# One output copy of each group moves from ScalarE to VectorE, and one low part of the last batch moves two slots earlier

## The chip, the core and the metric

The kernel runs on one core of a Trainium2 chip. Its time is the device time of one execution in microseconds (us). Engines go by the names of the profile: PE is TensorE (PEld its weight loads), ACT is ScalarE, DVE is VectorE, POOL is GpSimd, and SP is SyncE, which issues the DMAs here.

## What is computed

An attention with 32 inducing points over four batches of 12544 tokens of 128 channels, and a maxout layer on its result. Cut to what matters:

```python
def mab(q, kv):
    s = scale * (q @ kv.transpose(0, 2, 1))
    s = s - s.max(-1, keepdims=True)
    a = np.exp(s)
    a /= a.sum(-1, keepdims=True) + 1e-09
    return a @ kv
h = mab(I, x)            # 32 rows a batch
y = mab(x, h)            # as many rows as tokens
# then, with w1, w2, w3 of 128 x 768 and w_out of 768 x 128
h = np.maximum(np.maximum(y @ w1, y @ w2), y @ w3)
return h @ w_out
```

## The kernel before

A batch has 98 tiles of 128 tokens. They are taken in seven groups: one short group of two tiles and six full groups of 16. A full group is worked as four chunks `q` of 512 columns (a short one as one chunk of 256), so that a batch has 25 chunks and the program 100, numbered `c.n`. Each chunk has six slots `j`, one for each 128 of the 768 hidden channels: 600 slots in all, 24 for a full group. In this text a slot of a full group is numbered from 0 to 23 within it, and a stretch runs from the start of the first matmul of a group's slot 0 to that of the next group. There are 24 such stretches, six a batch.

The largest of three products is made with w2's product taken off: with weights `w1 - w2` PE makes a matmul into `pu` (L790), with `w3 - w2` one into `pv` (L800), ACT makes `ru`, the relu of `pu` (L809), DVE makes `h`, the larger of `pv` and `ru` (L830). What was taken off comes back through `w2 @ w_out`, once a chunk (L861). The second product, `h` by `w_out`, is made in two parts for accuracy: ACT rounds `h` to `hi` (L819), and `lows` is the rest, `h - hi`, made by POOL (L827) or, for a few slots, by DVE (L833). Six slots later PE adds `hi` by both parts of `w_out` and `lows` by the high part into `acc` (L862 to L864, in `stage2`). When a chunk's six slots are in, `finish` copies `acc` to `o` (L875) and SP sends it out (L876).

The order of the instructions is written out by hand. `main` goes through the slots: in each it calls `advance`, then a pending `finish`, then what a plan holds for this slot (steps of the two softmaxes, loads, sums), then `stage2`. `advance` issues for slot s: `pu` of slot s+1, `pv` of s, `ru` of s+1, `hi` of s-1, then on DVE `h` of s and behind it a low part that was put off from the call before, so that the low part of slot k stands behind `h` of slot k+2. A chunk's `finish` comes six slots after its last one; that of the first chunk (`q` = 0) of a full group stands at slot 12 of the group. At slot 2 of each stretch PE makes a burst: scores for the next group (L696), in the last batch for every other group; in batches 1 to 3 also scores and sums of the next batch (L366, L502). The other steps of the softmax stand between slots 3 and 15: DVE L709, L712, L714, L719, L726, L727, the transpose L739 and `pl` L745, ACT L716, L724 and `ph` L742.

`pu`, `pv` and `acc` have two PSUM banks each, `h` has five buffers, `o` three. `LOWVEC` and `LOWLAST` (L120, L121) hold the slots of a group whose low part DVE makes, `LOWLAST` for the last batch. Output copies are ACT's, save those of chunks 0 to 2 and half of the last chunk.

Of the kernel before, what the change touches and what calls it, by code (L numbers as in the profile page):

```python
# [25 lines left out]
def kernel(ctx, tc, x, xt, ind_t, w1, w2, w3, w_out, out):  # L26
    nc = tc.nc
# [90 lines left out]
        (16, 10, "t", 3, 6),  # L118
    )
    LOWVEC = (23, 0, 15, 18)  # L120
    LOWLAST = (23, 0, 9, 15, 18)  # L121
    UW = 2 * DF + C
    UQ = UW // NQ

# [556 lines left out]
    def sorted_(ap):  # L681

        return ap.rearrange("p (b a) -> p a b", a=2)

    def halves(ap):

        return ap.rearrange("p (a b) -> p a b", a=2)
# [147 lines left out]
    class Chunk:  # L835
# [7 lines left out]
        def low(self, k):  # L843
# [3 lines left out]
            if self.b == 0 and self.gi == 1:  # L847
                return NJ * self.q + k in LOWVEC[:1]
            return NJ * self.q + k in (LOWVEC if self.b + 1 < B else LOWLAST)

# [14 lines left out]

    def finish(c):
        at = groups[c.gi]["at"] + (c.q or 0) * c.w
        turns = [(nc.vector.tensor_copy if c.n < 3 else nc.scalar.copy, nc.sync)]
        if len(c.acc) > 1:

            turns = [(nc.vector.tensor_copy, nc.sync), (nc.scalar.copy, nc.scalar)]
        for (acc, cs), (copy, queue) in zip(c.acc, turns):
            o = op.tile([P, 512], F32, name="o", tag="o", bufs=3)
            w = cs.stop - cs.start
            copy(out=halves(o[:, :w]), in_=sorted_(acc[:, :w]))  # L875
            queue.dma_start(out=out[c.b, :, at + cs.start : at + cs.stop], in_=o[:, :w])  # L876
# [120 lines left out]
    def main():  # L997
        over = None
        for s in range(len(slots) + LAG + 1):

            if s >= LAG:
                spare[0] = bank_o[((s - LAG) // NJ + 1) % 2]
            if pipe["next"] <= s:
                advance()
            k = s // NJ + AHEAD
            if s % NJ == 4 and k < len(chunks):
                chunks[k].pT = probs(chunks[k])
            if over:
                finish(over)
                over = None  # L1010
            if s == len(slots) + LAG:
                break
            for f, args in plan[s]:
                f(*[state[a[1]] if isinstance(a, tuple) and a[0] == "state" else a for a in args])
            if s >= LAG:
                c, j = slots[s - LAG]
                stage2(c, j)
                if j == NJ - 1:
                    over = c
# [132 lines left out]
```

## Time and profile before

| | |
|---|---|
| median of 3 runs | 789.68 us (789.67 to 790.14) |
| the profiled execution | 790.35 us, of which the span of its instructions is 788.5 us |
| granted TensorE clock, mean | 0.999 of full speed |
| PE busy | 774.7 us, 98% of the span |
| PE weight loads busy | 626.4 us, 79% |
| ACT busy | 727.1 us, 92% |
| DVE busy | 639.4 us, 81% |
| POOL busy | 639.6 us, 81% |

Busy time is the union of the instructions' times, and an instruction's time includes what it takes to pass through its engine; the next one may start before it ends. A matmul of 512 columns is shown as 0.38 us long, and the next starts some 0.215 us after it. For such engines the distance from one start to the next tells more than the duration. "Idle before" is the time in which an engine had nothing running, with what released it.

### The profile page before, as it was taken

How to read it: one execution, taken by the hardware profiler on the slowest of the kernel's cores; microseconds unless marked ns; L12 is line 12 of the kernel's file. 1: busy time of each engine (PE TensorE's matmuls, PEld its weight loads, DVE VectorE, ACT ScalarE, POOL GpSimd, SP SyncE). 2: the span in 40 equal slices, each digit the busy share in tenths (PEclk: the TensorE clock that was granted, in tenths of full speed). 3: DMA queues.
4: the chain of work that ended last, by engine and by line, in shares of the span. 5: the costliest groups of instructions: out<-in, count | busy, mean ns of one | idle time of the engine just before them, and what ended most of it. 6: DMA issues, size and time to landing. Idle time of an engine off the chain costs nothing.

```text
span 788.5 us, 14348 instructions
## 1 busy us (share of the span) xinstructions
PE 774.7 (98%) x4567; PEld 626.4 (79%) x4567; DVE 639.4 (81%) x1071; ACT 727.1 (92%) x1529; POOL 639.6 (81%) x523
## 2 busy tenths in 40 slices
PE   8999999999999999999999999999999999999998
PEld 6768878878787787787878877878888788787887
DVE  5898978878877787887887878878888788888876
ACT  5789899999998999998998999999999999999996
POOL 1379879878788897887987978879879989888887
PEclk9999999999999999999999999999999999999999
DMA  9744325274542643543644336334223222222221
GB/s 355 293 148 126 100 91 178 62 249 161 189 139 65 200 131 101 188 123 108 217 137 132 114 103 195 120 114 134 71 79 96 74 81 81 68 87 73 69 81 53
DMA packets 52266, 102.24 MB, mean 130 GB/s; under 512 B 18144, under 2 KB 21344, under 8 KB 46944
## 3 DMA queue, kind: packets, MB, share of 16 engines
q1 hardware_dynamic: 52048, 101.21, 40.5%
q8 instruction: 36, 0.59, 0.3%
q14 instruction: 38, 0.31, 0.1%
q10 hardware_dynamic: 144, 0.13, 0.0%
HBM read 48.12 MB, written 25.69 MB: 94 GB/s over the span
## 4 chain that ended last, share of the span: by engine, by line
PE 56%; ACT 33%; POOL 3%; DMA 3%; DVE 2%; issue 1%; SPq 0%; POOLq 0%; ACTq 0%; DVEq 0%
ACT ru L809 14%; ACT hi L819 13%; PE pu L790 10%; PE acc L862 9%; PE pv L800 9%; PE acc L863 9%; PE acc L864 9%; PE aux L696 3%; POOL lows L827 3%; ACT o L875 2%; PE acc L502 2%; DMA raw<-in_w_dram 2%; PE aux L366 2%; PE acc L861 2%; ACT aux L449 1%
## 5 line engine op out<-in xcount | busy, mean ns | idle before, releaser
L827 POOL TENSOR_TENSOR lows<-h,hi 128x512 fp32r<-128x512 f32 (+1 forms) x504 | 624.4, 1275 | 112.4 <-ACT hi L819 109.3
L830 DVE TENSOR_TENSOR h<-pv,ru 128x512 f32<-128x512 f32 (+1 forms) x600 | 400.9, 673 | 123.8 <-PE pv L800 63.0
L809 ACT ACTIVATE ru<-pu 128x512 f32<-128x512 f32 (+1 forms) x600 | 407.0, 679 | 37.8 <-PE pu L790 37.5
L819 ACT CAST hi<-h 128x512 fp32r<-128x512 f32 (+1 forms) x596 | 416.3, 699 | 0.3 <-DVE h L830 0.2
L790 PE MATMUL pu<-pT,us 128*128 128x512 f32 (+1 forms) x600 | 229.2, 382 | 4.5 <-ACT ru L809 3.7
L800 PE MATMUL pv<-pT,us 128*128 128x512 f32 (+1 forms) x600 | 226.6, 378 | 1.6 <-DVE h L830 1.5
L862 PE MATMUL acc<-hi,wo_hi 128*128 128x512 f32 (+1 forms) x594 | 225.5, 380 | 0.0
L863 PE MATMUL acc<-hi,wo_lo 128*128 128x512 f32 (+1 forms) x594 | 222.6, 375 | 0.0
L864 PE MATMUL acc<-lows,wo_hi 128*128 128x512 f32 (+1 forms) x594 | 222.6, 375 | 0.0
L790 PEld LDWEIGHTS pu<-pT,us 128*128 128x128 f32 x600 | 113.2, 189 | 37.8 <-ACT ru L809 18.8
L862 PEld LDWEIGHTS acc<-hi,wo_hi 128*128 128x128 f32 x594 | 112.2, 189 | 21.9 <-issue 7.5
L800 PEld LDWEIGHTS pv<-pT,us 128*128 128x128 f32 x600 | 113.4, 189 | 19.6 <-DVE h L830 6.6
L864 PEld LDWEIGHTS acc<-lows,wo_hi 128*128 128x128 f32 x594 | 112.3, 189 | 15.3
L863 PEld LDWEIGHTS acc<-hi,wo_lo 128*128 128x128 f32 x594 | 112.3, 189 | 14.7
L833 DVE TENSOR_TENSOR lows<-h,hi 128x512 fp32r<-128x512 f32 x96 | 87.7, 913 | 0.8 <-ACT hi L819 0.8
L875 ACT COPY o<-acc 128x512 f32<-128x512 f32 (+1 forms) x96 | 65.3, 680 | 0.0
L861 PE MATMUL acc<-pT,us 128*128 128x512 f32 (+1 forms) x99 | 37.3, 376 | 0.0
L502 PEld LDWEIGHTS acc<-xg,aT 128*32 128x32 f32 x640 | 18.0, 110 | 9.6 <-issue 5.4
L696 PE MATMUL aux<-xT,hT 128*32 128x512 f32 x192 | 25.1, 603 | 0.0
L366 PE MATMUL aux<-xT,iT 128*32 128x512 f32 x184 | 24.1, 596 | 0.2 <-ACT pT L768 0.2
L502 PE MATMUL acc<-xg,aT 128*32 128x128 f32 x640 | 21.4, 273 | 0.1
L861 PEld LDWEIGHTS acc<-pT,us 128*128 128x128 f32 x99 | 18.7, 189 | 2.6 <-DVE hs L540 0.2
(163 smaller groups left out, 445.6 us busy)
## 6 DMA issues: line engine op xcount, KB each, us to landing
out_dram<-o SPq DMA_DIRECT2D x95, 256.0 KB, 2.2
xg<-in_x_dram SPq DMA_DIRECT2D x23, 1024.0 KB, 6.1
xT<-in_xt_dram SPq DMA_DIRECT2D x18, 1024.0 KB, 5.5
pT<-ph SPq DMA_DIRECT2D x190, 64.0 KB, 2.0
pT<-pl SPq DMA_DIRECT2D x190, 64.0 KB, 2.0
raw<-in_w_dram SPq DMA_DIRECT2D x3, 768.0 KB, 8.7
us<-uh SPq DMA_DIRECT2D x24, 52.0 KB, 1.9
us<-ul SPq DMA_DIRECT2D x24, 52.0 KB, 2.5
```

The lines of the kernel that those rows point to most:

```text
L790: nc.tensor.matmul(out=pu[:, :w], lhsT=state[c.b]["us"][:, 2 * j * P : (2 * j + 1) * P], rhs=turned(c.pT[:, :w]), start=True, stop=True,)
L800: nc.tensor.matmul(out=pv[:, : d.w], lhsT=state[d.b]["us"][:, (2 * j + 1) * P : (2 * j + 2) * P], rhs=turned(d.pT[:, : d.w]), start=True, ...
L809: nc.scalar.activation(out=halves(ru[:, :w]), in_=sorted_(pu[:, :w]), func=AF.Relu)
L819: nc.scalar.copy(out=hi[:, : c.w], in_=h[:, : c.w])
L827: nc.gpsimd.tensor_sub(**args)
L830: nc.vector.tensor_max(out=halves(h[:, : d.w]), in0=sorted_(pv[:, : d.w]), in1=halves(relus.pop(s)[:, : d.w]))
L833: nc.vector.tensor_sub(**low)
L861: nc.tensor.matmul(out=to, lhsT=us[:, 2 * DF :], rhs=turned(c.pT[:, cs]), start=True, stop=False)
L862: nc.tensor.matmul(out=to, lhsT=wo_hi[:, row_of(j), :], rhs=turned(c.hh[j][:, cs]), start=False, stop=False)
L863: nc.tensor.matmul(out=to, lhsT=wo_lo[:, row_of(j), :], rhs=turned(c.hh[j][:, cs]), start=False, stop=False)
L864: nc.tensor.matmul(out=to, lhsT=wo_hi[:, row_of(j), :], rhs=turned(c.hl[j][:, cs]), start=False, stop=(j == NJ - 1))
L875: copy(out=halves(o[:, :w]), in_=sorted_(acc[:, :w]))
```

## The change

`finish` lets VectorE copy the output of every chunk with `q` = 0, the first of each full group. In the last batch the slot 9 in the list of low parts on VectorE becomes slot 7: POOL makes that of slot 9, VectorE that of slot 7.

```diff
     LOWVEC = (23, 0, 15, 18)
-    LOWLAST = (23, 0, 9, 15, 18)
+    LOWLAST = (23, 0, 7, 15, 18)
...
     def finish(c):
         at = groups[c.gi]["at"] + (c.q or 0) * c.w
-        turns = [(nc.vector.tensor_copy if c.n < 3 else nc.scalar.copy, nc.sync)]
+        turns = [(nc.vector.tensor_copy if c.n < 3 or c.q == 0 else nc.scalar.copy, nc.sync)]
```

No other engine's order changes than those of ACT and DVE (POOL makes as many subtractions as before). On ACT, a full group in batches 1 to 3, at slot 12 (`pu_81` and `pu_82` are the two banks of `pu`, `acc_86` is one of `acc`):

```order
 L809 ACTIVATE ru<-pu_82 128x512
 L819 CAST hi<-h 128x512
-L875 COPY o<-acc_86 128x512
 L809 ACTIVATE ru<-pu_81 128x512
 L819 CAST hi<-h 128x512
```

The copy is gone from between `hi` and the next `ru`. On DVE, the same place (`aux_79` holds the scores of the next group, `rs` the reciprocal of their sums, `pv_83` and `pv_84` are the banks of `pv`):

```order
 L727 TENSOR_TENSOR aux_79<-aux_79,rs 128x512
 L830 TENSOR_TENSOR h<-pv_83,ru 128x512
+L875 COPY o<-acc_86 128x512
 L830 TENSOR_TENSOR h<-pv_84,ru 128x512
 L739 STREAM_TRANSPOSE aux_79<-aux_79 128x512
```

It stands there behind `h` of slot 12, ahead of `h` of slot 13 and of the transpose of the softmax. On DVE, a group of the last batch, from slot 8 to slot 13:

```order
 L830 TENSOR_TENSOR h<-pv_83,ru 128x512
 L830 TENSOR_TENSOR h<-pv_84,ru 128x512
+L833 TENSOR_TENSOR lows<-h,hi 128x512
 L719 TENSOR_REDUCE rs<-aux_80 128x16
 L830 TENSOR_TENSOR h<-pv_83,ru 128x512
 L830 TENSOR_TENSOR h<-pv_84,ru 128x512
-L833 TENSOR_TENSOR lows<-h,hi 128x512
 L726 RECIPROCAL rs<-rs 128x16
 L727 TENSOR_TENSOR aux_80<-aux_80,rs 128x512
 L830 TENSOR_TENSOR h<-pv_83,ru 128x512
+L875 COPY o<-acc_85 128x512
 L830 TENSOR_TENSOR h<-pv_84,ru 128x512
```

The low part leaves its place behind `h` of slot 11 for one behind `h` of slot 9, and the copy comes in behind `h` of slot 12, as in the other batches.

## Rows read from the trace of the kernel before

**Rows 1.** The page: busy times of PE and its weight loads, and the chain by engine

```profile
PE 774.7 (98%) x4567; PEld 626.4 (79%) x4567; DVE 639.4 (81%) x1071; ACT 727.1 (92%) x1529; POOL 639.6 (81%) x523
...
PE 56%; ACT 33%; POOL 3%; DMA 3%; DVE 2%; issue 1%; SPq 0%; POOLq 0%; ACTq 0%; DVEq 0%
```

**Rows 2.** Who waited for whom: us in total, times, the longest

```profile
PEld pu L790 <- ACT ru L809: 18.8, 49, 0.7
```

**Rows 3.** Two stretches: length, then each engine's busy us (instructions), clock, DMA

```profile
298.41:328.85 30.43, 30.13 (x173) 24.38 (x173) 24.87 (x41) 28.50 (x61) 25.14 (x21) 1.00 0.44 137
...
548.40:577.76 29.36, 29.36 (x169) 24.72 (x169) 24.42 (x42) 28.28 (x59) 25.42 (x21) 1.00 0.24 70
```

**Rows 4.** The chain of waits from 298 to 334: start, us, what

```profile
306.32 0.60 ACT ru L809
...
317.94 0.49 ACT o L875
```

**Rows 5.** Timeline of PE, end of the first stretch: start, us, engine, line, operation

```profile
326.98 0.38 PE L864 MATMUL acc<-lows,wo_hi 128*128 128x512 f32 x1
327.66 0.48 PE L790 MATMUL pu<-pT,us 128*128 128x512 f32 x1 [0.31 <-ACT ru L809]
327.98 0.38 PE L800 MATMUL pv<-pT,us 128*128 128x512 f32 x1
```

**Rows 6.** Groups by form: xcount, busy us, mean ns, idle before

```profile
L875 ACT COPY o<-acc 128x512 f32<-128x512 f32 x93 | 64.1, 689 | 0.0
```

**Rows 7.** Timeline of ACT, the same stretch, at slot 12

```profile
317.75 0.68 ACT L875 COPY o<-acc 128x512 f32<-128x512 f32 x1
318.23 0.70 ACT L809 ACTIVATE ru<-pu 128x512 f32<-128x512 f32 x1
...
320.22 0.70 ACT L742 CAST ph<-aux 128x512 fp32r<-128x512 f32 x1
```

**Rows 8.** Timeline of DVE, the same place

```profile
316.98 0.68 DVE L830 TENSOR_TENSOR h<-pv,ru 128x512 f32<-128x512 f32 x1
317.86 0.69 DVE L830 TENSOR_TENSOR h<-pv,ru 128x512 f32<-128x512 f32 x1 [0.20 <-PE pv L800]
318.47 0.72 DVE L739 STREAM_TRANSPOSE aux<-aux 128x512 f32<-128x512 f32 x1
...
320.02 0.69 DVE L830 TENSOR_TENSOR h<-pv,ru 128x512 f32<-128x512 f32 x1 [0.26 <-POOL lows L827]
```

**Rows 9.** Timeline of DVE, first group: one of its output copies

```profile
64.86 0.68 DVE L875 COPY o<-acc 128x512 f32<-128x512 f32 x1
```

**Rows 10.** Timeline of POOL at that time, merged

```profile
58.82 13.71 POOL L827 TENSOR_TENSOR lows<-h,hi 128x512 fp32r<-128x512 f32 x11
```

**Rows 11.** Timeline of DVE, the last batch, stretch from 640.50

```profile
653.07 0.68 DVE L719 TENSOR_REDUCE rs<-aux 128x16 f32<-128x512 f32 x1
653.67 0.68 DVE L830 TENSOR_TENSOR h<-pv,ru 128x512 f32<-128x512 f32 x1
...
655.23 1.32 DVE L833 TENSOR_TENSOR lows<-h,hi 128x512 fp32r<-128x512 f32 x1
...
657.35 1.28 DVE L830 TENSOR_TENSOR h<-pv,ru 128x512 f32<-128x512 f32 x2
```

**Rows 12.** Timeline of POOL in that stretch, three instructions merged

```profile
652.24 3.76 POOL L827 TENSOR_TENSOR lows<-h,hi 128x512 fp32r<-128x512 f32 x3
```

**Rows 13.** Timeline of PE in that stretch

```profile
655.18 0.38 PE L800 MATMUL pv<-pT,us 128*128 128x512 f32 x1
...
657.34 0.38 PE L790 MATMUL pu<-pT,us 128*128 128x512 f32 x1
658.09 0.48 PE L800 MATMUL pv<-pT,us 128*128 128x512 f32 x1 [0.37 <-DVE h L830]
```

**Rows 14.** Timeline of PE at the program's end

```profile
783.96 0.38 PE L864 MATMUL aux<-lows,wo_hi 128*128 128x256 f32 x1 [0.34 <-POOL lows L827]
```

## The prediction, before the changed kernel was run

> **What bounds the kernel now.** I read the page first, then the waits, the stretches, the chain of one stretch, and the timelines of each engine in it. The page says that PE is busy for 98% of the span [rows 1], which looks like a kernel with nothing left. But a matmul of 512 columns is shown as 0.38 us long while the next starts 0.215 us after it, so that share hides short waits. The other line of the page, the chain that ended last, is one third ACT [rows 1], and PE's weight load for `pu` waits 49 times for ACT's `ru` [rows 2].
>
> Of the 24 stretches of one full group each (24 slots), eight are 30.43 us long; the one from 298.41 to 328.85 stands for them [rows 3]. ACT is busy for 28.50 of its 30.43 us. It idles once, while PE computes scores and sums in a burst, and from 306.32 on the chain runs through ACT, instruction behind instruction, and ACT's output copy at 317.94 lies on it [rows 4]. (The timeline shows the same copy at 317.75; the chain counts it from the end of what precedes it.) The chain leaves ACT where PE must wait: the matmul into `pu` starts 0.68 us after the one ahead of it, where 0.215 us is the pace, and the next needs 0.32 us. PE so loses 0.47 + 0.10 = 0.57 us [rows 5]. `pu` has two banks; PE may not write one until ACT's `ru` has read it. Then PE goes on to the next burst, and the cycle closes. So in these stretches what ACT sheds ahead of that wait shortens the cycle, up to what PE waits.
>
> **The change, part by part.** *The copy leaves ACT.* 23 copies of 128x512 move: one for each of 24 full groups, less that of chunk 1, which VectorE makes already. A copy is shown as 689 ns [rows 6], but the next ACT instruction starts 0.48 us after it (317.75 to 318.23, rows 7), and that is what ACT gains. It is bounded by 0 and 0.48 us a group. For twelve stretches (the eight, the second of batch 1, the fifth of batch 2 and the first of batches 2 and 3) PE's waits exceed 0.48 us, so I take it whole: 12 x 0.48 = 5.76 us. [...]
>
> Of the other stretches of batches 1 to 3, one (548.40) has PE busy without a break [rows 3]; I give it nothing. Four hold fewer of these waits; I take 0.38 us each, the mean of the 49 [rows 2], between 0 and 0.48: 4 x 0.38 = 1.52 us.
>
> *The copy joins VectorE.* It stands behind `h` of slot 12, so it would start at 317.58 where that one starts at 316.98 [rows 8] and the pace of VectorE is 0.60 us. `h` of slot 13 goes from 317.86 to 318.18, the transpose from 318.47 to 318.79. `h` of slot 15 started at 320.02 after an idle time, which takes up what is left: the delay is over. What waits for them? ACT's `ph` would now come at 319.74 rather than 320.22 [rows 7], and the transpose ends at 318.79 + 0.72 = 319.51. So the copy costs nothing here; the margin is 0.23 us, and past it ACT would wait and give the gain back. The copy's input is long done, its output DMA keeps its place on SP, and three `o` buffers cover a shift of tenths.
>
> How long does it last? VectorE made three such copies early on, and the one at 64.86 took 0.68 us [rows 9] while POOL ran eleven subtractions without a gap [rows 10]. That matters because the low part that VectorE computes is slow under POOL: 1.32 us instead of 0.68, ending 0.55 us after POOL's instruction ends at 656.00 [rows 11, 12]. The copy does not wait that way.
>
> *The low part at slot 7 instead of 9, last batch.* In the stretch from 640.50 it stood between `h` of slots 11 and 12, waited for POOL, and with two more instructions behind it `h` of slot 12 came at 657.35. PE's `pv` of slot 14, due 0.215 us after 657.34, started at 658.09: 0.53 us lost, and 0.10 to restart [rows 11, 13]. Now it issues where 653.07 stands, waits for POOL's first instruction of rows 12 (3.76 / 3 = 1.25 us, so to 653.5) and ends near 654.05. `h` of slot 10 goes from 653.67 to 654.6 and ends at 655.3; `pv` of slot 12 was due at 655.18 [rows 13], so PE loses about 0.1 + 0.1 there. Then `h` of slot 12 comes near 656.7, 0.6 us earlier than before; the copy takes that 0.6 us, and `h` of slot 13 is where it was. The old wait of 0.63 is a wait of 0.2. Three of the last six stretches have the old wait; 3 x 0.43 = 1.29 us, between 0 (the wait only moves) and 1.9 us (it goes). Of the others PE has no wait to lose, and 0.48 us of ACT buys nothing there. What is late next in them is PE itself.
>
> *The end.* The last products wait 0.34 us for POOL [rows 14], whose instructions in the last group start after ACT's `hi`; ACT arrives earlier, so I take 0.34 us, between 0 and 0.48.
>
> The sum is 5.76 + 1.52 + 1.29 + 0.34 = 8.91 us. The profiled execution took 790.35 us, 1.85 more than its span; less 8.91 it is 781.44. It lies 0.67 above the median of the three runs, 789.68, so I predict **780.8 us**.
>
> **The rivals.** *Slower: the copy waits for POOL after all.* VectorE's low part is the row for it [rows 11]; against it are the early copies [rows 9, 10]. A wait of half a POOL instruction, 0.64 us, exceeds the margin of 0.23 by 0.41, so a steady stretch gains 0.07 rather than 0.48 us: 0.8 us in all. In eight groups VectorE has no idle time there (two with two softmaxes, six of the last batch), and PE pays the 0.64: 5.1 us. That is 4.3 us slower, 794.0 us. It decides from a copy longer than 0.68 + 0.23 = 0.91 us.
>
> *No change: PE is the bound, as its 98% says.* Its waits would be ones it always has, the time 789.7 us. Against it are the chain through ACT and the lost 0.57 us [rows 4, 5]. [...]
>
> *Half: the next thing in line takes the rest.* If `h` of slot 13 or the transpose runs only some 0.2 us later than I reckon, ACT waits for it in every group. Then 0.24 us a stretch are left, 12 x 0.24 = 2.9 us, and if the last batch's wait only moves and the four others halve (0.8), with the end (0.34) the gain is about 4 us: 785.6 us.
>
> **How the numbers follow.** A measurement of this kernel can tell about 0.2%, 1.6 us, from no change. I give the forecast 0.72, half 0.13, no change 0.06, the slower rival 0.09. Faster by over 0.2% is the first two, 0.85; within it 0.06; slower 0.09. The range begins where the other stretches of batches 1 to 3 also give all 0.48 us, the last batch's waits go, and some of its stretches gain 0.48: 777.5 us. It reaches past the half case, to 786.0, and leaves out no change and slower.
>
> **What would show it.** Steady stretches should be 29.95 us long instead of 30.43, with ACT still the chain and PE's wait before the burst about 0.1 instead of 0.47 us. The VectorE copies should last 0.68 us; a mean over 0.9 means the slower rival. ACT's `ph` should follow its predecessor without idle time. In the last batch the wait of `pv` for `h` should be at slot 12, short, and gone from slot 14. I am wrong if PE's wait vanishes while the stretch keeps its length, or if ACT's idle time during the burst grows by what the copy freed.

## The result, and the profile after

The change made the kernel slower. Its 20 runs have a median of 805.58 us (790.62 to 813.95) beside 790.04 us (789.46 to 790.65) before; the ratio is 1.0079, 95% interval 1.0052 to 1.0106. The ratio is taken over the nine runs nearest the fastest, since a comparison leaves disturbed runs out; here the scatter is the change's own, as the experiments show, so the median of all 20, 2.0% above before, says more. The forecast was 780.8 us.

The profiled execution is the fastest of the 20: 790.62 us, span 788.8 us, beside 790.35 and 788.5 before. So it shows gains and losses that nearly cancel. The page of the changed kernel, the lines that answer to [rows 1]:

```profile
PE 772.5 (98%) x4567; PEld 630.0 (80%) x4567; DVE 662.8 (84%) x1094; ACT 717.5 (91%) x1506; POOL 642.1 (81%) x523
...
PE 86%; ACT 5%; DMA 4%; issue 2%; SPq 1%; DVE 1%; POOL 0%; DVEq 0%; ACTq 0%
```

ACT's third of the chain has gone, as meant. 23 copies left ACT (1529 to 1506 instructions) and joined DVE (1071 to 1094). But DVE's busy time grew by 23.4 us, more than 23 copies at 0.68 us, 15.6. The groups by form show what else grew (xcount, busy us, mean ns, idle before):

```profile
L833 DVE TENSOR_TENSOR lows<-h,hi 128x512 fp32r<-128x512 f32 x96 | 102.7, 1070 | 0.8 <-ACT hi L819 0.8
...
L875 DVE COPY o<-acc 128x512 f32<-128x512 f32 x25 | 17.0, 680 | 0.0
```

Before, VectorE's low parts read so:

```profile
L833 DVE TENSOR_TENSOR lows<-h,hi 128x512 fp32r<-128x512 f32 x96 | 87.7, 913 | 0.8 <-ACT hi L819 0.8
```

There are as many now, but their durations sum to 15.0 us more. (Durations overlap, so this and the copies are more than 23.4.) The waits of the changed kernel (us in total, times, the longest), beside [rows 2]:

```profile
PEld pv L800 <- DVE h L830: 16.3, 28, 2.5
...
ACT hi L819 <- DVE h L830: 7.1, 5, 1.9
...
PEld pu L790 <- ACT ru L809: 5.4, 22, 0.4
PE pv L800 <- DVE mx L434: 4.2, 2, 2.1
```

The wait for ACT's `ru` fell from 18.8 to 5.4 us. In its place PE's weight loads wait 28 times for DVE, for up to 2.5 us (6.6 us in 18 waits before), and ACT five times, for up to 1.9 us. The row that names `mx` (L434) is misleading: that reduction, 0.14 us long, only stands behind the instruction that was late. Three stretches that all took 30.43 us before, and one piece of the last (length, then busy time of PE, PEld, DVE, ACT and POOL, clock, DMA, as in [rows 3]):

```profile
107.19:139.28 32.09, 29.99 (x173) 24.53 (x173) 28.09 (x43) 28.22 (x59) 25.07 (x21) 1.00 0.42 134
139.28:169.18 29.90, 29.90 (x174) 24.59 (x172) 25.64 (x42) 27.87 (x60) 25.30 (x21) 1.00 0.42 137
487.23:521.00 33.77, 31.67 (x173) 25.71 (x173) 28.88 (x43) 29.67 (x62) 26.76 (x22) 0.95 0.41 131
517.36:520.77 3.41, 3.41 (x9) 2.70 (x8) 2.54 (x5) 3.31 (x8) 2.23 (x2) 0.50 0.15 40
```

The second is what was forecast: 29.90 us, PE busy throughout. The first holds one wait of PE of 2.10 us. The third holds the same wait, and 1.2 us after it TensorE's granted clock stood at 0.50 of full speed for 3.41 us. Matmuls followed each other at 0.43 instead of 0.215 us there; 33.77 less 32.09 is what that cost, 1.7 us. Here is what happened in the first stretch, on DVE, POOL, ACT and PE in turn (timeline: start, us, engine, line, operation, and idle time before):

```profile
130.95 0.69 DVE L830 TENSOR_TENSOR h<-pv,ru 128x512 f32<-128x512 f32 x1 [0.27 <-PE pv L800]
131.56 3.94 DVE L833 TENSOR_TENSOR lows<-h,hi 128x512 fp32r<-128x512 f32 x1
135.43 0.68 DVE L830 TENSOR_TENSOR h<-pv,ru 128x512 f32<-128x512 f32 x1
136.03 0.14 DVE L434 TENSOR_REDUCE mx<-mx 128x1 f32<-128x5 f32 x1
...
127.49 7.46 POOL L827 TENSOR_TENSOR lows<-h,hi 128x512 fp32r<-128x512 f32 x6
...
131.48 0.73 ACT L819 CAST hi<-h 128x512 fp32r<-128x512 f32 x1
...
136.14 0.62 ACT L819 CAST hi<-h 128x512 fp32r<-128x512 f32 x1 [1.93 <-DVE h L830]
...
133.68 0.38 PE L790 MATMUL pu<-pT,us 128*128 128x512 f32 x1
136.16 0.48 PE L800 MATMUL pv<-pT,us 128*128 128x512 f32 x1 [2.10 <-DVE mx L434]
```

VectorE's low part of slot 15 takes 3.94 us. POOL meanwhile does those of slots 14, 16 and 17 without a gap (six instructions in 7.46 us, 1.24 us from start to start, the last three from 131.22 to 134.95), and VectorE's ends at 135.50, 0.55 us after POOL's last. This is the delay of 0.55 us that [rows 11] and [rows 12] show, behind three instructions of POOL instead of a part of one. `h` of slot 18 stands behind it on DVE, so ACT's `hi` waits 1.93 us and PE's `pv` loses 2.27 us.

Before, POOL paused at that place. The same stretch of the kernel before, DVE, POOL and ACT:

```profile
132.31 1.17 DVE L833 TENSOR_TENSOR lows<-h,hi 128x512 fp32r<-128x512 f32 x1
...
127.87 5.06 POOL L827 TENSOR_TENSOR lows<-h,hi 128x512 fp32r<-128x512 f32 x4
133.20 2.65 POOL L827 TENSOR_TENSOR lows<-h,hi 128x512 fp32r<-128x512 f32 x2 [0.28 <-ACT hi L819]
...
132.37 0.75 ACT L819 CAST hi<-h 128x512 fp32r<-128x512 f32 x1
```

POOL ended slot 14 at 132.93 and then waited 0.28 us for ACT's `hi` of slot 16. In this pause VectorE's low part got in, and ended at 133.48, again 0.55 us after POOL. Now ACT is some 0.5 us earlier in the stretch: its `hi` of slot 16 ends at 132.21, 25.02 us after the stretch's start (133.12 and 25.53 before). That is 0.28 us before POOL's subtraction of slot 14 ends (132.49), and POOL goes on without a pause.

That alone does not decide it. In the stretch from 139.28 ACT leads as much, and VectorE gets in all the same (DVE, POOL):

```profile
163.62 1.48 DVE L833 TENSOR_TENSOR lows<-h,hi 128x512 fp32r<-128x512 f32 x1
...
160.77 6.71 POOL L827 TENSOR_TENSOR lows<-h,hi 128x512 fp32r<-128x512 f32 x5
```

Let a low part on VectorE that takes 3 us or more, because POOL goes from one subtraction straight to the next, be called a shut-out. The profile of after has four that before does not have (at 131.6, 262.1, 353.1 and 511.6; one more, at 80.7, both have).

### The profile page after: what moved, and what is told of

The parts are those of the page before. It is cut to its first block, busy times and chain, and to the rows that moved or that the text cites. A ratio compares the mean times of both kernels' runs of the same rounds, so it can differ in the third digit from the quotient of the medians.

```text
span 788.8 us, 14395 instructions
## 1 busy us (share of the span) xinstructions
PE 772.5 (98%) x4567; PEld 630.0 (80%) x4567; DVE 662.8 (84%) x1094; ACT 717.5 (91%) x1506; POOL 642.1 (81%) x523
## 4 chain that ended last, share of the span: by engine, by line
PE 86%; ACT 5%; DMA 4%; issue 2%; SPq 1%; DVE 1%; POOL 0%; DVEq 0%; ACTq 0%
PE pv L800 15%; PE acc L862 15%; PE pu L790 15%; PE acc L863 14%; PE acc L864 14%; PE aux L696 3%; PE acc L502 2%; PE aux L366 2%; PE acc L861 2%; ACT ru L809 2%; ACT hi L819 2%; DMA xg<-in_x_dram 1%; DMA pT<-ph 1%; DVE h L830 1%; DMA xT<-in_xt_dram 1%
## 5 line engine op out<-in xcount | busy, mean ns | idle before, releaser
L809 ACT ACTIVATE ru<-pu 128x512 f32<-128x512 f32 (+1 forms) x600 | 391.3, 653 | 40.5 <-PE pu L790 40.2
L819 ACT CAST hi<-h 128x512 fp32r<-128x512 f32 (+1 forms) x596 | 400.8, 673 | 7.6 <-DVE h L830 7.1
L790 PE MATMUL pu<-pT,us 128*128 128x512 f32 (+1 forms) x600 | 226.8, 378 | 0.2
L833 DVE TENSOR_TENSOR lows<-h,hi 128x512 fp32r<-128x512 f32 x96 | 102.7, 1070 | 0.8 <-ACT hi L819 0.8
L875 ACT COPY o<-acc 128x512 f32<-128x512 f32 (+1 forms) x73 | 47.6, 652 | 0.0
```

The costliest lines, as they stand in the source:

```text
L790: nc.tensor.matmul(out=pu[:, :w], lhsT=state[c.b]["us"][:, 2 * j * P : (2 * j + 1) * P], rhs=turned(c.pT[:, :w]), start=True, stop=True,)
L809: nc.scalar.activation(out=halves(ru[:, :w]), in_=sorted_(pu[:, :w]), func=AF.Relu)
L819: nc.scalar.copy(out=hi[:, : c.w], in_=h[:, : c.w])
L833: nc.vector.tensor_sub(**low)
```

## The experiments

The theory: relieving ACT takes away POOL's pause, and VectorE's low part of slot 15 is then shut out in some groups. The rivals: the copy on VectorE delays or disturbs what follows it there; or the low part at slot 7 does. The first four were run on one chip (before: 790.06, 789.71 to 790.74).

**The copy's move alone.** Against the change:

```diff
-    LOWLAST = (23, 0, 7, 15, 18)
+    LOWLAST = (23, 0, 9, 15, 18)
```

> The copy on VectorE, the low part of the last batch back at slot 9. Theory (pause lost): ACT, relieved of the copy, has hi of slot 16 ready before POOL ends slot 14, so POOL goes on without the pause of some 0.3 us in which VectorE's low part of slot 15 used to come in; it is then held off for two or three POOL instructions. Expected: low parts over 2 us in three to six groups of batches 1 to 3, times scattered from about 790 to 815 us as with the change. Rival (the low part at slot 7 does it): no low part over 2 us but the one near 80.6 us that was there before, and about 782 to 784 us.

Measured: 800.23 us (794.32 to 811.63 in four), ratio 1.0103 (1.0064 to 1.0142). The profiled run, the slowest, has eight new shut-outs, more than the three to six expected, and six stretches of 3.41 us at clock 0.50, and its 24 stretches sum to 748.86 us instead of 727.74. The stretch that went well in the profile of after, 163.62, is shut out in this one (DVE, POOL):

```profile
163.91 3.96 DVE L833 TENSOR_TENSOR lows<-h,hi 128x512 fp32r<-128x512 f32 x1
...
161.09 6.23 POOL L827 TENSOR_TENSOR lows<-h,hi 128x512 fp32r<-128x512 f32 x5
```

POOL's five take 6.23 us here and 6.71 there: where VectorE gets in, POOL's next subtraction lasts 1.75 us instead of 1.27.

**The low part alone.** Against the change:

```diff
-        turns = [(nc.vector.tensor_copy if c.n < 3 or c.q == 0 else nc.scalar.copy, nc.sync)]
+        turns = [(nc.vector.tensor_copy if c.n < 3 else nc.scalar.copy, nc.sync)]
```

> The low part of the last batch at slot 7, every output copy where it was before. Theory: batches 1 to 3 as before, no low part over 2 us but the one near 80.6 us, no scatter, and the last batch some 1.3 us shorter: 788 to 789.5 us. Rival (the low part at slot 7 does it): scatter up to 810 us.

Measured: 789.27 us (788.90 to 789.65 in ten), ratio 0.9989 (0.998 to 0.9999). No new shut-out, no scatter: the fault is the copy's half.

**ACT relieved, VectorE not loaded.**

```diff
     def finish(c):
+        if c.q == 0 and c.n >= 3:
+            return
...
-        turns = [(nc.vector.tensor_copy if c.n < 3 or c.q == 0 else nc.scalar.copy, nc.sync)]
+        turns = [(nc.vector.tensor_copy if c.n < 3 else nc.scalar.copy, nc.sync)]
```

> The output of the first chunk of 23 groups is neither copied nor sent, so neither ACT nor VectorE has that work; the low part of the last batch at slot 7. Theory: ACT's relief is what takes POOL's pause, so low parts over 2 us appear in some groups of batches 1 to 3 and the times scatter over more than 5 us, from about 788 up. Rival (VectorE, with one copy more, comes late): no such low part, no scatter, 779 to 782 us.

Measured: 805.78 us (802.0 to 809.77), ratio 1.0199 (1.0161 to 1.0236), with seven new shut-outs and four falls of the clock. On the page:

```profile
L833 DVE TENSOR_TENSOR lows<-h,hi 128x512 fp32r<-128x512 f32 x96 | 107.5, 1120 | 0.8 <-ACT hi L819 0.8
```

23 copies fewer in the kernel (and their output DMAs), and it is 2% slower. No copy stood on VectorE, so the copy there is not the cause; ACT's lead is enough.

**Both engines copy.** VectorE copies as in the change, and ACT copies the same product to a tile that nothing reads:

```diff
             copy(out=halves(o[:, :w]), in_=sorted_(acc[:, :w]))
+            if c.q == 0 and c.n >= 3:
+                o2 = op.tile([P, 512], F32, name="o2", tag="o2", bufs=1)
+                nc.scalar.copy(out=halves(o2), in_=sorted_(acc))
```

> VectorE copies as in the change, and ACT copies the same products too, into a tile that nobody reads; the low part of the last batch at slot 7. Theory: without ACT's relief the pause is there, so no low part over 2 us but the one near 80.6 us, no scatter, 788 to 790.5 us. Rival (VectorE's added copy does it): low parts over 2 us in three to six groups, scatter up to 810 us.

Measured: 800.60 us (800.1 to 801.4), ratio 1.0133 (1.0118 to 1.0149). No new shut-out, no scatter, the clock full throughout: that part held. The time missed, because the edit brought a wait of its own (waits; DVE; ACT):

```profile
ACT o L878 <- DVE o L875: 9.8, 19, 1.1
...
133.19 0.71 DVE L833 TENSOR_TENSOR lows<-h,hi 128x512 fp32r<-128x512 f32 x1
...
127.91 0.58 ACT L878 COPY o<-acc 128x512 f32<-128x512 f32 x1 [0.37 <-DVE o L875]
```

ACT's copy waits 0.37 us for VectorE's in a steady stretch, which is 30.87 us long. ACT is so even later than before, POOL's pause is 0.73 us, and VectorE's low part takes 0.71 us in it. That adds a point on the other side: the later ACT, the shorter that low part.

If POOL's unbroken run is the cause, then either the low part of slot 15 has to leave VectorE, or POOL must be given less to do ahead of it. Four lists of slots, each against the change and on one chip (before: 790.04, 789.7 to 791.68), edit the line for batches 1 to 3:

```diff
-    LOWVEC = (23, 0, 15, 18)
+    LOWVEC = (23, 0, 7, 15, 18)
```

> The change, and slot 7 added to VectorE's low parts in batches 1 to 3 as in the last batch (five of 24 instead of four). Theory: POOL has one subtraction less ahead of slot 15, so it has caught up with ACT by then and pauses for hi; VectorE's low part of slot 15 gets in. No low part over 2 us but the one near 80.6 us, no scatter, steady stretches about 29.9 us, 780 to 784 us (VectorE has 0.6 us and a wait of up to 1.3 us more a group). Rival (the scatter has another cause than POOL's missing pause): scatter over more than 5 us stays.

Measured: 783.80 us (782.95 to 784.11), ratio 0.9919 (0.9902 to 0.9935). Steady stretches are 29.93 us, their low parts of slot 15 take 1.28 to 1.30 us, and there is no new shut-out. But POOL does not pause for `hi`, as was expected: it makes seven subtractions from 155.56 to 164.77 without a gap, and VectorE's low part of 161.09 gets in between two of them. What the fifth slot does is to shorten the time by which ACT's `hi` of slot 16 is ahead of POOL, to 0.09 us there from 0.28 in the change.

```diff
-    LOWVEC = (23, 0, 15, 18)
+    LOWVEC = (23, 0, 18)
```

> The change, and the low part of slot 15 made by POOL in batches 1 to 3, so that VectorE has no such part inside POOL's train. Theory: no low part over 2 us but the one near 80.6 us, no scatter; POOL works 1.25 us longer a group, of some 4.5 us that it idles: 779 to 783 us. If POOL becomes late for the buffers of h, PE waits and it is 784 to 789 us, still without scatter. Rival: scatter stays.

Measured: 784.50 us (784.47 to 784.59), ratio 0.993 (0.9916 to 0.9945). With POOL doing slot 15 too, the low part of slot 18 waits for POOL, mostly 1.59 to 1.83 us long and twice 2.03 or 2.04, and steady stretches are 30.0 to 30.5 us.

```diff
-    LOWVEC = (23, 0, 15, 18)
+    LOWVEC = (23, 0, 1, 18)
```

> The change, and in batches 1 to 3 VectorE makes the low part of slot 1 instead of that of slot 15; it then stands just behind PE's burst, where POOL idles. Theory: no low part over 2 us but the one near 80.6 us, no scatter; 780 to 784 us. Rival: scatter stays.

Measured: 790.68 us (789.69 to 796.26 in ten), ratio 1.0017 (0.9999 to 1.0034). A miss: the low part at slot 1 makes VectorE late behind the burst (ACT's `hi` idles 0.27 us for `h` at 118.71), and PE loses 0.41 us at `pu` before the next one, so that a steady stretch is 30.51 us. And its last batch, where slot 15 is still VectorE's, has a shut-out in the last group (DVE, POOL, PE):

```profile
775.33 3.73 DVE L833 TENSOR_TENSOR lows<-h,hi 128x512 fp32r<-128x512 f32 x1
...
769.76 8.74 POOL L827 TENSOR_TENSOR lows<-h,hi 128x512 fp32r<-128x512 f32 x7
...
779.71 0.48 PE L800 MATMUL pv<-pT,us 128*128 128x512 f32 x1 [1.89 <-DVE h L830]
```

The end is the same: 769.76 + 8.74 + 0.55 is 779.05, and 775.33 + 3.73 is 779.06.

```diff
-    LOWVEC = (23, 0, 15, 18)
+    LOWVEC = (23, 0, 17, 18)
```

> The change, and in batches 1 to 3 VectorE makes the low part of slot 17 instead of that of slot 15; POOL's train then ends with slot 16, since 17 and 18 are VectorE's, and the low part comes in behind it. Theory: no scatter; the low part of slot 17 waits for the end of slot 16 in every group (1.2 to 2 us long), which PE feels by some tenths: 782 to 786 us. Rival: scatter stays.

Measured: 784.54 us (783.48 to 785.02), ratio 0.9929 (0.9914 to 0.9944). VectorE's low part of slot 17 takes some 1.6 us in steady stretches, and 2.12 and 2.13 us where one more subtraction of POOL goes ahead of it; there is no new shut-out.

The last four were run on one chip (before: 790.18, 789.5 to 791.41). They ask which fifth slot is best and whether the gain is the fifth low part's or the copy's.

```diff
-    LOWVEC = (23, 0, 15, 18)
+    LOWVEC = (23, 0, 9, 15, 18)
```

> The change, and slot 9 (not 7) added to VectorE's low parts in batches 1 to 3. By the theory POOL still has one subtraction less ahead of slot 15, so no low part over 2 us but the one near 80.6 us and no scatter; but the part stands where the last batch had it before, between h of slot 11 and the softmax's product, and the copy follows: PE should wait for h at slot 14 for some tenths, 784 to 788 us. If it waits no more than with slot 7: 783 to 784 us.

Measured: 788.04 us (787.79 to 789.14 in ten), ratio 0.9975 (0.9965 to 0.9984): no shut-out, but a steady stretch is 30.27 us.

```diff
-    LOWVEC = (23, 0, 15, 18)
+    LOWVEC = (23, 0, 7, 15, 18)
...
-        turns = [(nc.vector.tensor_copy if c.n < 3 or c.q == 0 else nc.scalar.copy, nc.sync)]
+        turns = [(nc.vector.tensor_copy if c.n < 3 else nc.scalar.copy, nc.sync)]
```

> Slot 7 among VectorE's low parts in every batch as in the run before this series that did so, but every output copy where it was before the change. What is left of that run's gain is then due to the low part. Theory: the gain is ACT's relief, which needs both; without the relief ACT sets the pace as before: 788 to 790 us, no scatter. Rival (the fifth low part on VectorE is the gain): 783 to 785 us.

Measured: 789.98 us (789.56 to 790.66 in ten), ratio 0.9998 (0.9989 to 1.0008). The fifth low part by itself gains nothing.

```diff
-    LOWVEC = (23, 0, 15, 18)
+    LOWVEC = (23, 0, 5, 15, 18)
```

> The change, and slot 5 added to VectorE's low parts in batches 1 to 3. Theory: as with slot 7, no low part over 2 us but the one near 80.6 us, no scatter. It stands two slots further from the copy, so in groups with more work on VectorE (two softmaxes) PE should wait less at slot 12: 782 to 784 us; if POOL is not yet busy enough behind the burst to lose by it, no difference from slot 7.

Measured: 782.54 us (781.5 to 782.69), ratio 0.9899 (0.9884 to 0.9914). This is the best version, 1.0% faster than the kernel before. One steady stretch, then its low part of slot 15 and POOL at that time:

```profile
136.62:166.55 29.93, 29.93 (x173) 24.52 (x173) 26.04 (x43) 27.99 (x59) 24.28 (x20) 1.00 0.45 142
...
160.99 1.30 DVE L833 TENSOR_TENSOR lows<-h,hi 128x512 fp32r<-128x512 f32 x1
...
156.73 7.95 POOL L827 TENSOR_TENSOR lows<-h,hi 128x512 fp32r<-128x512 f32 x6
```

The version with slot 7 in both lists (the edit of the fifth run) was run once more, to stand beside these:

> The change with slot 7 among VectorE's low parts in batches 1 to 3 once more, for its interval: 783 to 784.5 us in every run, 0.7 to 0.9% under the kernel before. If POOL's train can still shut VectorE out by chance, single runs at 786 us and more.

Measured: 783.62 us (783.36 to 784.0), ratio 0.9916 (0.9901 to 0.9931). With the low part at slot 7 in all batches, the copy on VectorE rather than ACT is worth 789.98 less 783.62, 6.4 us.

## Why the prediction was wrong

**The gain was there.** Of the twelve stretches costed at 0.48 us each, the eight without a shut-out gained 0.47 to 0.54, 0.52 in the mean. The copies take 0.680 us in the mean, as the one in [rows 9]. PE's wait before the burst is 0.10 us where it was 0.47, and ACT's `ph` follows its predecessor without idle time. VectorE took the copy as reckoned.

**The four others** were given 0.38 us each; counted from full group to full group, with the short one between them, two gained 0.37 and 0.36, two nothing: 0.72 in place of 1.52 us.

**The last batch** was given 1.29 us with 1.9 as its upper end, and gained 1.93: its six stretches are 27.28, 26.98, 28.81, 26.95, 27.96 and 25.68 us long, where they took 27.70, 27.40, 28.89, 27.76, 28.04 and 25.80. In the stretch from 642.59 on DVE:

```profile
655.16 0.98 DVE L833 TENSOR_TENSOR lows<-h,hi 128x512 fp32r<-128x512 f32 x1
...
656.66 1.27 DVE L830 TENSOR_TENSOR h<-pv,ru 128x512 f32<-128x512 f32 x2
...
659.33 0.68 DVE L875 COPY o<-acc 128x512 f32<-128x512 f32 x1
```

The low part of slot 7 gets through in 0.98 us. PE's wait at slot 14 is gone, and one of 0.08 to 0.17 us at slot 12 is left in three of the stretches. The two halves of the change need each other here: the first five of these stretches gain 0.84 us with the low part alone, lose 0.74 with the copy alone and gain 1.80 with both. **The end** gained 0.30 us of 0.34.

Without the shut-outs the sum would be 12 x 0.52 + 0.72 + 1.93 + 0.30 = 9.2 us, where 8.91 was forecast. No run shows this sum as such.

**The step that failed** is the bound of the first term, "It is bounded by 0 and 0.48 us a group", with the sentence on VectorE behind the copy, "the delay is over". Both look at the copy's neighbours and stop at slot 13. ACT runs some 0.5 us earlier for the rest of the group, up to the burst; the next thing that this reaches is POOL, whose pause ahead of slot 16 (0.25 to 0.30 us in the steady stretches) came from ACT's lateness. What lived in that pause was VectorE's low part of slot 15. The prediction had its delay in hand [rows 11, 12] and used it only for the copy (as 0.64 us, half an instruction of POOL's) and for slots 9 and 7 of the last batch (to the end of one instruction). It did not ask which of VectorE's other low parts depend on a pause, nor whether several of POOL's instructions may go ahead. The trace of before held the answer to the second (DVE, POOL, in the first batch):

```profile
80.62 3.63 DVE L833 TENSOR_TENSOR lows<-h,hi 128x512 fp32r<-128x512 f32 x1
...
78.70 5.00 POOL L827 TENSOR_TENSOR lows<-h,hi 128x512 fp32r<-128x512 f32 x4
```

It takes 3.63 us and ends 0.55 us after POOL's run. PE was in its burst then (scores and sums, 79.94 to 83.74) and lost nothing, so that no list of waits showed it. So the bound of the first term had to reach below nothing: a shut-out stretch of 30.43 us became some 1.66 us longer, 3.34 with the fall of the clock.

In the profiled run three shut-out stretches lost 1.66, 1.67 and 3.34 us, the one from 239.29 lost 0.60 on balance; together 7.27 us. The other stretches gained 4.85 in batches 1 to 3 and 1.93 in the last, the end 0.30, and the start lost 0.06. That makes 0.25 us slower; it was 0.27. The typical run is worse, and none of the change's slower runs was profiled; the nearest, the copy alone at 811.63 us, has eight shut-outs and six falls of the clock, and its stretches are 21.1 us longer than before.

**The rivals.** The slower one had the right sign by the wrong road: the copy never waits for POOL (0.680 us in the mean, where 0.91 would have decided). *No change* falls with the stretches of 29.90 us, *half* with ACT's `ph`, which does not wait.

**Which of VectorE's instructions waited.** The subtraction `h - hi` did, the copy from PSUM did not. In the profile of after the low part at 131.56 took 3.94 us, while three of POOL's instructions went ahead of it, and the 25 copies of 128x512 took 0.672 to 0.682 us each.

**What stays open.** Why VectorE gets in at POOL's boundary in one group and not in the next. In the profiles of after, of the copy alone and of ACT relieved, the low part was issued 0.27 to 0.37 us after POOL's slot 14 began in most groups of batches 1 to 3, and took 1.48 to 1.56 us in some, 3.94 to 4.05 in others. The outcome goes with ACT's lead, the time by which `hi` of slot 16 is ready before POOL's slot 14 ends. In the fourteen profiles together POOL went from slot 14 straight to slot 16 in 105 groups with a low part of slot 15 on VectorE. With a lead of 0.06 to 0.13 us, as in most groups of the versions with slot 5 or 7, none of 58 was shut out (issued 0.37 to 0.81 us after slot 14 began); with 0.26 us or more, 20 of 47 were. A late issue alone is no protection: with slot 1 in place of 15, in the last group, the low part was issued 0.57 us after slot 14 began and was shut out, with a lead of 0.53 us. But at nearly the same issue and lead others got in, so what decides among the 47 is not known. Nor is it settled why the clock fell after some waits of PE and not after others of the same length (32.09 and 33.77 us both hold 2.27 us).

## What to carry to other kernels

When an engine is made earlier, look for a pause that its lateness gave to a third engine, and for what gets its turn only in that pause; the price of losing it can be far more than the gain (here 1.66 us of a stretch and more, against 0.52), and is no delay of one instruction (three of POOL's went ahead, 3.94 us). Where two engines compete, let the term's lower bound lie below nothing, and time several runs: a profile of the fastest shows the least of it. Giving POOL one subtraction less, early in the group, kept the copy's gain of some 0.5 us a stretch (782.54 us), though the pause did not come back; ACT's lead over POOL was shorter (some 0.09 us, where the change had 0.28).

## What the runs showed of the hardware

A VectorE subtraction with both inputs in SBUF, 0.68 us alone, took 3.94, 3.04, 3.95 and 3.94 us in the four new shut-outs of the profile of after (and 3.96 us at 163.91 with the copy alone, 3.96 at 131.31 with ACT relieved) beside POOL subtractions that ran back to back. It ended 0.55 us after the last of POOL's that went ahead of it. At like timing it took 1.48 us (163.62 in the profile of after). A copy of 128x512 from PSUM on the same engine kept 0.68 us throughout (0.672 to 0.682 in that profile). So one kernel ran between 790.62 and 813.95 us, with mean granted clocks from 1.0 to 0.983: some waits of PE of about 2 us were followed by 3.41 us at clock 0.50 (one of 2.10 us, 1.2 us before the clock fell at 517.36).
